# Linear attention with a maxout FFN on one core: a planner with other DMA times, other ranks, query exponentials in two steps

## The chip, the cores and the metric

The kernel runs on one core of a Trainium2 chip. The metric is the device time in microseconds (us) of one execution; the kernel before took 721.54 us, the median of three runs (720.34 to 723.81). The engines are named as the profile names them: PE (TensorE) with its weight loads PEld, DVE (VectorE), ACT (ScalarE), POOL (GpSimd), and SP, whose queue issues the DMAs.

## The reference

Eight batches of eight heads, 576 positions, head dimension 64, all in float32. Queries go through a softmax over the head dimension, keys through a softmax over the sequence. `kv` is a 64x64 matrix for each head, and the result, laid out as 4608 tokens x 512, goes through a maxout layer with three weight matrices and an output matrix.

```
q_s = exp(q - max(q, -1));  q_s /= sum(q_s, -1) + 1e-9
k_s = exp(k - max(k, seq)); k_s /= sum(k_s, seq) + 1e-9
kv  = einsum('bhsd,bhse->bhde', k_s, v)
x   = einsum('bhsd,bhde->bhse', q_s, kv)       -> 4608 x 512
h   = max(x @ w1, x @ w2, x @ w3)              w1..w3: 512 x 768
out = h @ w_out                                w_out: 768 x 512
```

## The kernel before, in words

**Work.** A pair is two heads of one batch: four pairs for each batch, 32 in all. For a pair the kernel takes the largest key of each column, exponentiates the keys, builds `kv` on PE (L489), scales it into a block-diagonal matrix (`bdf` for batches 0 and 1, `bdh` and `bdl` after; L505, L509), and multiplies the normalized queries by it (L639) into a piece of `x`: `x` for the first 512 positions, `left` for the 64 that remain. ACT casts the piece to its high part (L642) and DVE takes the low part (L644).

**Two kinds of batches.** Batches 0 and 1 are *turned*: PE transposes the keys (L419, L423), DVE reduces them (L428 to L430), ACT exponentiates (L434, L435), PE turns them back (L442, L444), ACT or DVE copies them out (L451); queries are transposed on PE (L612, L616) and copied into `qf` by ACT (L621, L623). Batches 2 to 7 are *plain*: DVE folds the keys (L459 to L461), POOL reduces over partitions (`kma`, L464), DVE subtracts (L467), ACT exponentiates (L474); queries turn by a DVE transpose and eight DMAs. A turned pair's queries are exponentiated either row by row on ACT (ten times an ACTIVATE of 128x64 and the read of its sum, L543; pairs in `Q_BY_ACT`), or by one subtraction (L548), one ACTIVATE of 128x640 (L563) and a sum on DVE (L565). L567, L568 and L571 normalize.

**FFN.** There are nine chunks of 512 token rows, one for each batch and one for the left-over rows. For a chunk there are 18 gate groups of four *trios* (a trio is three matmuls of 128x512, of low and high parts, L669), whose results ACT copies (L678) and DVE maximizes (L681); then ACT casts the high part of the hidden rows (L684), DVE takes the low part `h_l` (L687, a step that the planner may give to DVE or POOL), and 24 trios make the output (L707). The weights come as 24 slices of 512 KB of 64-bit numbers, each of which ACT, DVE and POOL turn into float parts (L320 to L348, POOL at L333); gate groups wait for their slice.

**Order.** The instructions' order on each engine is planned when the kernel is built. Every step of a stream names its engine, its cost in us and what it waits for (`Step`), and `Streams.run` gives each engine, whenever it comes free in the planner's clock, the ready step with the lowest rank. Ranks come from `AT`, `STEP`, `FIRST`, `CHUNK`, `SLICES_AT` and `SLICE_STEP`; the DMAs' times from the cost on SP (`"S"`), from `kb` and from `DMA_RATE`. At run time an engine works its list in that order and waits by semaphores. The small transposes, `kv` and left-over products of PE go through one PSUM tile `ps` of four quarters; the program's semaphores put all accesses to `ps` in the order in which they stand in the program. Gate groups go through four PSUM tiles `pf`.

Of the kernel before, what the change touches and what calls it, by code (L numbers as in the profile page):

```python
# [25 lines left out]
SIGNAL = 0.22  # L26
AHEAD = 0.5
DMA_LANDS = 2.0
DMA_RATE = 300.0
WAIT = 0.02  # L30

FIRST, CHUNK, SLICE = 27.0, 66.0, 2.7

AT = (7.3, 14.2, 18.2, 22.2, 39.0, 46.0, 63.0, 66.0)
STEP = (1.4, 2.8)
SLICES_AT, SLICE_STEP, SLICE_HI, SLICE_LO = 11.4, 0.18, 1.23, 1.56
# [41 lines left out]
class Streams:  # L78
# [16 lines left out]
    def ready(self, s, engine):  # L95
# [57 lines left out]

    def issue(self, t, e, c, s):
        step = s[4]
        end = t + c
        self.clock[e] = end
        if e in step.port:
            self.port = end
        if step.kb:  # L160
            self.queues = max(self.queues, end) + step.kb / DMA_RATE
            end = self.queues + DMA_LANDS
        s[3], s[5] = end, e
        if step.gives:
# [10 lines left out]
def linear_attention_then_maxout_ffn(  # L175
# [26 lines left out]
    nc = tc.nc  # L202
# [78 lines left out]
    st = Streams({"pf": 4, "pa": 3, "ps": 4, "keT": 1, "hp": NJ, "tmp": 3, "ke": 2, "qe": 2, "qf": 1, "qt": 2, "tb": 1, "qT": 2, "qhl": 1}, {"pf": in_pf})  # L281
    late_pools, turn_pools = [], []
    quarters = ps.tile([P, 4, P], F32, name="ps")
    small = (quarters[:, i % 4, :] for i in itertools.count())

# [66 lines left out]
    class Pair:  # L352
# [19 lines left out]
        def k_load(self):  # L372
            if self.b:
                prev = self.ago("ksub") if self.n >= NP + 2 else None
                if self.turned:
                    yield Step("S", 1.1, [prev], kb=256)
                    for hh in range(2):
                        nc.sync.dma_start(out=self.kt[:, 0:4, hh, :], in_=head_rows(k, self.b, 2 * self.g + hh))
                else:
                    yield Step("S", 0.55, [prev], kb=256)  # L380
                    nc.sync.dma_start(out=self.kt[:, :, 0:4, :], in_=main_rows(k, self.b, self.hs))
                yield Step("S", 0.5, gives=("k", self.n), kb=32)
                nc.sync.dma_start(
                    out=self.kt[0:LEFT, 4] if self.turned else self.kt[0:LEFT, :, 4, :], in_=left_rows(k, self.b, self.hs)
                )

        def v_load(self):
            if self.b:
                prev = self.ago("kv") if self.n >= NP + 2 else None
                for hh in range(2):  # L390
                    yield Step("S", 0.6, [prev], kb=128)
                    nc.sync.dma_start(out=self.vt[:, hh, 0:4, 0:D], in_=head_rows(v, self.b, 2 * self.g + hh))
                yield Step("S", 0.5, gives=("v", self.n), kb=32)
                nc.sync.dma_start(out=self.vt[0:LEFT, :, 4, 0:D], in_=left_rows(v, self.b, self.hs))

        def q_load(self):
            if self.b == 0:
                return
            if self.turned:
                prev = self.ago("qsub") if self.n >= NP + 2 else None  # L400
                self.qt = qbuf[self.m]
                yield Step("S", 0.55, [prev], kb=256)
                nc.sync.dma_start(out=self.qt[:, :, 0:4, :], in_=main_rows(q, self.b, self.hs))
                yield Step("S", 0.5, gives=("q", self.n), kb=32)
                nc.sync.dma_start(out=self.qt[0:LEFT, :, 4, :], in_=left_rows(q, self.b, self.hs))
            else:
                yield Step("S", 0.55, ["turn"], gives=("q", self.n), take=[("qt", self.n)], kb=288)
# [111 lines left out]
        def q_steps(self):  # L519
# [6 lines left out]
            if self.turned:  # L526
# [34 lines left out]
            if not by_act:  # L561
# [86 lines left out]
    class Chunk:  # L648
# [47 lines left out]
        def second(self, t):  # L696
# [38 lines left out]
    def first_loads():  # L735
# [143 lines left out]
```

## Time and profile before

| | us |
|---|---|
| median of three runs | 721.54 (720.34 to 723.81) |
| the profiled execution | 724.52 |
| its span in the trace | 722.4 |
| PE busy | 690.8 (96%) |
| DVE busy | 404.8 (56%) |
| ACT busy | 256.5 (36%) |
| POOL busy | 58.4 (8%) |

The profiled execution took 724.52 us, 3.0 more than the median; its trace spans 722.4 us. PE is the engine that is busy nearly throughout, so a wait of another engine counts only where PE waits for it. The stage up to 62.76 us holds most of PE's idle time.

### The profile page before, as it was taken

The page shows a single profiled execution, that of the slowest core. Times are in us where ns is not written, and L with a number is a line of the kernel's source. Part 1 is how long each engine was busy: PE and PEld are TensorE (multiplying, and loading weights), DVE is VectorE, ACT ScalarE, POOL GpSimd, SP SyncE. Part 2 cuts the span into 40 slices and gives each one's busy share as a digit, 9 for nine tenths or more (in the row PEclk, how much of TensorE's full clock was granted, in tenths as well). Part 3 has the DMA queues.
Part 4 walks back from the last instruction along what each step waited for, and adds up shares of the span by engine and source line. Part 5 has one row for each costly group of instructions (what it writes and reads, how often), then busy time and mean ns, then how long its engine had stood idle before and what let it go on. Part 6 is the DMA issues. An engine that isn't in the chain of part 4 may idle for free.

```text
span 722.4 us, 9841 instructions
## 1 busy us (share of the span) xinstructions
PE 690.8 (96%) x3528; PEld 553.5 (77%) x3528; DVE 404.8 (56%) x806; ACT 256.5 (36%) x610; POOL 58.4 (8%) x68
## 2 busy tenths in 40 slices
PE   3789999899999999999999999999999999999997
PEld 2557777677787887788878887888888888888886
DVE  6779997689988985675467646723222102211220
ACT  5878886333344324322342234212311111111111
POOL 2222432201000000000001000000000000000000
PEclk9989999999999999999999999999999999999999
DMA  7938414443445412530154005300100010000002
GB/s 212 257 110 252 134 61 135 141 104 99 110 125 155 113 46 69 143 109 1 33 146 126 18 25 149 83 1 10 66 1 0 15 44 0 1 33 26 1 0 59
DMA packets 86417, 58.07 MB, mean 80 GB/s; under 512 B 53344, under 2 KB 77920, under 8 KB 86368
## 3 DMA queue, kind: packets, MB, share of 16 engines
q1 hardware_dynamic: 86368, 57.44, 28.1%
q8 instruction: 28, 0.46, 0.3%
q14 instruction: 21, 0.17, 0.1%
HBM read 40.89 MB, written 9.44 MB: 70 GB/s over the span
## 4 chain that ended last, share of the span: by engine, by line
PE 85%; DVE 6%; DMA 3%; ACT 2%; SPq 2%; issue 1%; POOL 0%; DVEq 0%; ACTq 0%
PE pf L669 60%; PE pf L707 18%; PE ps L489 3%; PE pa L639 3%; ACT qe L543 1%; DMA kt<-in_k_dram 1%; PE ps L639 1%; DMA wst<-in_moe_w_dram 1%; SPq L589 1%; DVE ke L467 1%; PE pa L612 0%; DVE x L644 0%; DVE tb L576 0%; DMA qt<-in_q_dram 0%; SPq L757 0%
## 5 line engine op out<-in xcount | busy, mean ns | idle before, releaser
L669 PE MATMUL pf<-x,wh 128*128 128x512 f32 x1152 | 361.1, 395 | 1.1 <-DVE x L644 1.1
L669 PEld LDWEIGHTS pf<-x,wh 128*128 128x128 f32 x1152 | 218.0, 189 | 50.5 <-DVE x L644 1.7
L669 PE MATMUL pf<-x,wl 128*128 128x512 f32 x576 | 232.1, 403 | 0.9 <-ACT x L642 0.9
L681 DVE TENSOR_TENSOR m<-pf,m 128x512 f32<-128x512 f32 x108 | 74.3, 688 | 185.6 <-PE pf L669 185.0
L669 PEld LDWEIGHTS pf<-x,wl 128*128 128x128 f32 x576 | 109.2, 190 | 26.7 <-ACT x L642 1.1
L684 ACT CAST h_h<-m 128x512 fp32r<-128x512 f32 x54 | 33.5, 621 | 208.0 <-DVE m L681 208.0
L707 PE MATMUL pf<-ol,h_h 128*128 128x512 f32 x216 | 89.1, 412 | 0.0
L707 PE MATMUL pf<-oh,h_l 128*128 128x512 f32 x216 | 84.6, 392 | 0.0
L707 PE MATMUL pf<-oh,h_h 128*128 128x512 f32 x216 | 84.3, 390 | 0.0
L678 ACT COPY m<-pf 128x512 f32<-128x512 f32 x54 | 31.6, 586 | 52.2 <-PE pf L669 51.9
L687 DVE TENSOR_TENSOR h_l<-m,h_h 128x512 fp32r<-128x512 f32 x54 | 38.0, 704 | 20.7 <-ACT h_h L684 20.6
L707 PEld LDWEIGHTS pf<-ol,h_h 128*128 128x128 f32 x216 | 40.6, 188 | 9.0 <-issue 0.5
L707 PEld LDWEIGHTS pf<-oh,h_l 128*128 128x128 f32 x216 | 40.5, 188 | 8.9
L707 PEld LDWEIGHTS pf<-oh,h_h 128*128 128x128 f32 x216 | 40.7, 188 | 7.6 <-issue 0.5
L464 POOL PARTITION_ALL_REDUCE kma<-km x24 | 20.0, 832 | 305.3 <-DVE km L461 166.5
L669 PE MATMUL pf<-left,wh 128*128 128x512 f32 x144 | 44.3, 389 | 0.0
L712 ACT COPY m<-pf 128x512 f32<-128x512 f32 x36 | 21.1, 586 | 62.2 <-PE pf L707 61.3
L333 POOL TENSOR_TENSOR wst<-wx,wst 128x512 int32<-128x512 int32 x24 | 33.6, 1400 | 89.2 <-DVE wx L329 38.9
L576 DVE STREAM_TRANSPOSE tb<-qt 128x576 f32<-128x576 f32 x24 | 30.5, 1271 | 11.3 <-DMA qT<-tb 10.7
L669 PEld LDWEIGHTS pf<-left,wh 128*128 128x128 f32 x144 | 27.0, 188 | 5.6
L489 PEld LDWEIGHTS ps<-vt,ke 128*64 128x64 f32 (+1 forms) x560 | 18.9, 137 | 14.8 <-issue 5.0
L563 ACT ACTIVATE qt<-qt 128x576 f32<-128x576 f32 x24 | 16.5, 688 | 36.9 <-DVE qt L558 36.8
(110 smaller groups left out, 690.3 us busy)
## 6 DMA issues: line engine op xcount, KB each, us to landing
wst<-in_moe_w_dram SPq DMA_DIRECT2D x18, 512.0 KB, 4.2
out_dram<-m SPq DMA_DIRECT2D x32, 256.0 KB, 2.2
vt<-in_v_dram SPq DMA_DIRECT2D x56, 128.0 KB, 3.0
qt<-in_q_dram SPq DMA_DIRECT2D x24, 288.0 KB, 3.1
qT<-tb SPq DMA_DIRECT2D x192, 36.0 KB, 1.9
kt<-in_k_dram SPq DMA_DIRECT2D x24, 256.0 KB, 3.1
wst<-in_moe_w_out_dram SPq DMA_DIRECT2D x6, 512.0 KB, 3.3
q<-in_q_dram SPq DMA_DIRECT2D x8, 256.0 KB, 4.6
```

Source lines behind the costliest of these rows:

```text
L333: nc.gpsimd.tensor_add(out=low.bitcast(I32), in0=x.bitcast(I32), in1=low.bitcast(I32))
L464: nc.gpsimd.partition_all_reduce(kma, km, P, bass_isa.ReduceOp.max)
L489: nc.tensor.matmul(out=kv[r, :nv], lhsT=ke[rows, s, hh, :], rhs=self.vt[rows, hh, s, 0:nv], start=(s == 0), stop=(s == 4),)
L576: nc.vector.transpose(out=tb.rearrange("p e (c s) -> p s e c", s=QS), in_=self.qt.rearrange("p s (e c) -> p s e c", e=2))
L639: nc.tensor.matmul(out=xT, lhsT=l, rhs=r[:, cs], start=(i == 0), stop=(i == last))
L669: nc.tensor.matmul(out=ps, lhsT=l[:, cc, js], rhs=r, start=(cc == 0 and t == 0), stop=(cc == NC - 1 and t == 2))
L678: nc.scalar.copy(out=m, in_=self.m.pop((j, 0)))
L681: nc.vector.tensor_max(out=m, in0=self.m.pop((j, i)), in1=m)
L684: nc.scalar.copy(out=h, in_=m)
L687: unit[e].tensor_sub(out=lo, in0=m, in1=h.bitcast(F32))
L707: nc.tensor.matmul(out=po, lhsT=l, rhs=r[:, j, :], start=(j == 0 and i == 0), stop=(j == NJ - 1 and i == 2))
L712: nc.scalar.copy(out=o, in_=po)
```

## The change

All effective edits are to the planner's numbers, to the split of two steps, and to one PSUM ring. (1) DMA steps cost 0.64 us on SP for each DMA in place of 0.5 to 0.6; the planner's rate is 356 KB per us, and 0.62 of that up to 16 us, in place of 300; the left-over loads count as 50 KB and head-wise loads as 400 or 200. (2) The planner's engine clocks start at 0.72 to 4.0 us and not at 0. (3) `FIRST` goes from 27 to 22.7, `CHUNK` from 66 to 71.1, and `AT`, `STEP`, `SLICE_STEP` and `SLICE_HI` change. (4) The fourth pair's queries are loaded ahead of its keys, values and two weight slices. (5) Row-wise query exponentials are two steps of five rows. (6) Pairs 2 and 3 leave `Q_BY_ACT`. (7) Small PE results use three quarters of `ps` and not four; the fourth belongs to `keep_warm`, which with `WARM_TO` = 0 issues nothing.

```
-DMA_RATE = 300.0
+DMA_RATE, DMA_FIRST, DMA_AT_FIRST = 356.0, 0.62, 16.0
-FIRST, CHUNK, SLICE = 27.0, 66.0, 2.7
+WARM_FROM, WARM_TO, WARM_IDLE, WARM_COST = 4.2, 0.0, 0.3, 0.22
+FIRST, CHUNK, SLICE = 22.7, 71.1, 2.7
-AT = (7.3, 14.2, 18.2, 22.2, 39.0, 46.0, 63.0, 66.0)
-STEP = (1.4, 2.8)
+AT = (7.3, 14.2, 20.3, 22.2, 41.7, 48.7, 66.4, 62.3)
+STEP = (0.7, 3.92)
-FIRST_LOADS = 'kKqQvVwkqKQwvVkqwvkqvw'
+FIRST_LOADS = 'kKqQvVwkqKQwvVkqwqkvvw'
-Q_BY_ACT = (0, 1, 2, 3, 5, 6, 7)
+Q_BY_ACT = (0, 1, 5, 6, 7)
...
-        self.clock = dict.fromkeys("SAVGT-", 0.0)
+        self.clock = {"S": 0.72, "A": 2.2, "V": 4.0, "G": 3.0, "T": 0.0, "-": 0.0}
...
-            self.queues = max(self.queues, end) + step.kb / DMA_RATE
+            begun = max(self.queues, end)
+            self.queues = begun + step.kb / DMA_RATE / (DMA_FIRST if begun < DMA_AT_FIRST else 1.0)
...
-    small = (quarters[:, i % 4, :] for i in itertools.count())
+    small = (quarters[:, i % 3, :] for i in itertools.count())
...
-                    yield Step("S", 1.1, [prev], kb=256)
+                    yield Step("S", 1.28, [prev], kb=400)
...
-                    yield Step("A", rows * 0.33, take=[("qe", n)], gives=("qsub", n))
+                    yield Step("A", 5 * 0.33, take=[("qe", n)])
...
                     for hh in range(2):
+                        if hh:
+                            yield Step("A", 5 * 0.33, gives=("qsub", n))
                         for s in range(5):
...
-            yield Step("V", 0.28)
+            yield Step("V", 0.34)
```

Lines of the changed kernel stand 18 to 20 further down (L434 is L452, L543 is L563, L639 is L659, L669 is L689). Four places show what moves.

The first place is ACT's list from its first exponential on: `keT` are the turned keys, `qe` the queries, `wst` and `wh` a weight slice, `bdf` the scaled `kv`. Before:

```order
L543 ACTIVATE qe,qs_134<-q_98,qm_133 128x64 x10
L434 ACTIVATE keT,ks<-pa,km_217 128x512
L435 ACTIVATE keT,ks<-ps,km_217 128x64
L337 ACTIVATE wst<-wst 128x512
L341 CAST wh_79<-wx 128x4x128
L451 COPY ke<-pa 128x512
L451 COPY ke<-ps 64x128
L337 ACTIVATE wst<-wst 128x512
L621 COPY qf<-pa 128x512
L543 ACTIVATE qe,qs_136<-q_98,qm_135 128x64 x10
L341 CAST wh_80<-wx 128x4x128
```

And of the change, the same place:

```order
L452 ACTIVATE keT,ks<-pa,km_216 128x512
L453 ACTIVATE keT,ks<-ps,km_216 128x64
L563 ACTIVATE qe,qs_134<-q_98,qm_133 128x64 x5
L355 ACTIVATE wst<-wst 128x512
L563 ACTIVATE qe,qs_134<-q_98,qm_133 128x64 x5
L359 CAST wh_79<-wx 128x4x128
L523 ACTIVATE bdf_100<-ps,rk 64x64 x2
L563 ACTIVATE qe,qs_136<-q_98,qm_135 128x64 x5
L355 ACTIVATE wst<-wst 128x512
L641 COPY qf<-pa 128x512
L452 ACTIVATE keT,ks<-pa,km_303 128x512
L453 ACTIVATE keT,ks<-ps,km_303 128x64
```

The first keys' exponential (L434, now L452) moved ahead of the first queries', whose ten rows are now in two halves with a weight slice's step between, and the second `bdf` and `keT` no longer stand behind twenty rows.

The second place is PE about the third pair's `x` (`bdf_100`; `pa` and `ps` are the PSUM tiles of its 512 and 64 columns). Before:

```order
L639 MATMUL pa<-qf,bdf_100 128x512
L669 MATMUL pf<-x_86,wl_82 128x512
L669 MATMUL pf<-x_86,wh_79 128x512 x2
L442 MATMUL pa<-ident,keT 128x128 x4
L444 MATMUL ps<-ident,keT 64x128
L639 MATMUL ps<-qf,bdf_100 128x64
```

And of the change:

```order
L659 MATMUL pa<-qf,bdf_100 128x512
L659 MATMUL ps<-qf,bdf_100 128x64
L460 MATMUL pa<-ident,keT 128x128 x4
L462 MATMUL ps<-ident,keT 64x128
L632 MATMUL pa<-ident,qe 128x128 x4
L636 MATMUL ps<-ident,qe 128x64
```

The left-over product, which stood behind a trio and the next keys' transposes, now follows the main product directly.

The third place is PE at the first `kv` products of the plain batches (`vt0_92` and `vt1_93`, 128x65 in the trace; the number behind `pf` tells the gate group). Before:

```order
L489 MATMUL ps_130<-vt0_92,ke_1463 64x65 x10
L669 MATMUL pf_1482<-x1_756,wl0_82 128x512
L669 MATMUL pf_1482<-x1_756,wh0_79 128x512 x2
L669 MATMUL pf_1522<-x1_756,wl1_83 128x512
L669 MATMUL pf_1522<-x1_756,wh1_80 128x512 x2
L669 MATMUL pf_1522<-x1_756,wl1_83 128x512
L669 MATMUL pf_1522<-x1_756,wh1_80 128x512 x2
L489 MATMUL ps_130<-vt1_93,ke_1512 64x65 x10
```

And of the change:

```order
L507 MATMUL ps_130<-vt0_92,ke_1455 64x65 x10
L689 MATMUL pf_1468<-x1_712,wl0_82 128x512
L689 MATMUL pf_1468<-x1_712,wh0_79 128x512 x2
L689 MATMUL pf_1506<-x1_712,wl1_83 128x512
L689 MATMUL pf_1506<-x1_712,wh1_80 128x512 x2
L689 MATMUL pf_1506<-x1_712,wl1_83 128x512
L689 MATMUL pf_1506<-x1_712,wh1_80 128x512 x2
L689 MATMUL pf_1506<-x1_712,wl1_83 128x512
L689 MATMUL pf_1506<-x1_712,wh1_80 128x512 x2
L689 MATMUL pf_1506<-x1_712,wl1_83 128x512
L689 MATMUL pf_1506<-x1_712,wh1_80 128x512 x2
L507 MATMUL ps_130<-vt1_93,ke_1498 64x65 x10
```

Two more trios stand between the first and the second of these products.

The fourth place is POOL from the last clearing of buffers on (`kma` is the reduction over partitions, `h_l` the low part of hidden rows; ISA without names is a step that sets POOL up for the instruction that follows). Before:

```order
L789 MEMSET bdh_1435 128x128
L789 MEMSET bdl_1437 128x128
L789 MEMSET bdl_1439 128x128
L464 ISA
L464 ISA kma<-km 128x128 x24
```

And of the change:

```order
L482 ISA
L482 ISA kma<-km 128x128 x10
L707 ISA
L707 TENSOR_TENSOR h_l<-m,h_h 128x512
L482 ISA
L482 ISA kma<-km 128x128 x5
L707 ISA
L707 TENSOR_TENSOR h_l<-m,h_h 128x512
L482 ISA
L482 ISA kma<-km 128x128 x4
L707 ISA
L707 TENSOR_TENSOR h_l<-m,h_h 128x512
```

The 24 reductions stood in one row; now six `h_l` stand among them, five of them followed by a new set-up for the reductions, and each after a set-up of its own.

## Rows read from the trace of the kernel before

**Rows 1.** The page, parts 1 and 5: span, busy time, one group.

```profile
span 722.4 us, 9841 instructions
PE 690.8 (96%) x3528; PEld 553.5 (77%) x3528; DVE 404.8 (56%) x806; ACT 256.5 (36%) x610; POOL 58.4 (8%) x68
L687 DVE TENSOR_TENSOR h_l<-m,h_h 128x512 fp32r<-128x512 f32 x54 | 38.0, 704 | 20.7 <-ACT h_h L684 20.6
```

**Rows 2.** PE's waits, first 80 us: us in total, times, longest.

```profile
PE pa L442 <- ACT keT L434: 9.0, 2, 5.5
PE pa L419 <- DMA k<-in_k_dram: 4.5, 1, 4.5
PE ps L489 <- ACT qf L623: 2.8, 1, 2.8
```

**Rows 3.** Stretches: length, busy us by engine, granted clock, DMA share.

```profile
0.00:62.76 62.76, 41.68 (x239) 28.97 (x239) 47.74 (x118) 46.55 (x178) 16.33 (x23) 0.95 0.71 193
62.76:133.00 70.24, 70.24 (x362) 55.42 (x363) 59.86 (x117) 51.74 (x136) 22.14 (x22) 1.00 0.42 137
35.00:40.00 5.00, 2.24 (x23) 1.81 (x23) 4.25 (x10) 4.65 (x16) 1.19 (x1) 0.71 0.14 37
40.00:45.00 5.00, 4.78 (x16) 2.87 (x14) 2.69 (x9) 2.40 (x9) 0.10 (x1) 0.60 0.54 173
55.00:116.00 61.00, 60.15 (x339) 46.87 (x337) 58.78 (x110) 49.09 (x133) 19.82 (x14) 1.00 0.50 157
```

**Rows 4.** PE in order of time: start, length; idle before, releaser.

```profile
4.47 1.08 PE L419 MATMUL pa<-ident,k 128*128 128x128 f32 x4 [4.47 <-DMA k<-in_k_dram]
11.37 1.12 PE L442 MATMUL pa<-ident,keT 128*128 128x128 f32 x4 [5.51 <-ACT keT L434]
22.04 1.11 PE L442 MATMUL pa<-ident,keT 128*128 128x128 f32 x4 [3.50 <-ACT keT L434]
29.93 0.79 PE L669 MATMUL pf<-x,wl 128*128 128x512 f32 x1
37.98 1.54 PE L489 MATMUL ps<-v,ke 128*64 128x64 f32 x20 [2.76 <-ACT qf L623]
62.76 0.72 PE L669 MATMUL pf<-x,wh 128*128 128x512 f32 x2 [0.85 <-DVE x L644]
136.96 0.80 PE L489 MATMUL ps<-vt,ke 128*64 128x65 f32 x20 [1.67 <-ACT ke L474]
138.50 0.40 PE L669 MATMUL pf<-x,wl 128*128 128x512 f32 x1
139.19 0.39 PE L669 MATMUL pf<-x,wl 128*128 128x512 f32 x1
141.80 0.80 PE L489 MATMUL ps<-vt,ke 128*64 128x65 f32 x20 [1.76 <-ACT bdh L505]
295.44 0.30 PE L639 MATMUL ps<-q_l,bdh 128*128 128x64 f32 x1 [1.47 <-DVE bdl L509]
```

**Rows 5.** ACT in order of time, the first stage.

```profile
10.23 0.33 ACT L543 ACTIVATE qe<-q,qm 128x64 f32<-128x64 f32 x1
10.56 0.66 ACT L434 ACTIVATE keT<-pa,km 128x512 f32<-128x512 f32 x1
```

**Rows 6.** DVE in order of time: the start, the first plain pair.

```profile
7.11 0.68 DVE L428 TENSOR_REDUCE km<-pa 128x1 f32<-128x512 f32 x1
12.70 1.86 DVE L571 TENSOR_TENSOR qe<-qe,qs 128x640 f32<-128x640 f32 x1
20.91 0.82 DVE L571 TENSOR_TENSOR qe<-qe,qs 128x640 f32<-128x640 f32 x1
135.31 0.83 DVE L467 TENSOR_TENSOR ke<-kt,kma 128x640 f32<-128x640 f32 x1 [5.51 <-POOL kma L464]
```

**Rows 7.** POOL in order of time: its first slice and its first reduction.

```profile
12.58 1.29 POOL L333 TENSOR_TENSOR wst<-wx,wst 128x512 int32<-128x512 int32 x1 [9.59 <-DVE qs L567]
134.55 0.72 POOL L464 PARTITION_ALL_REDUCE kma<-km  x1 [5.82 <-issue]
```

More of the change, by code (lines that the diff above doesn't have):

```diff
@@ L28 @@
 DMA_LANDS = 2.0
-DMA_RATE = 300.0
+DMA_RATE, DMA_FIRST, DMA_AT_FIRST = 356.0, 0.62, 16.0
 WAIT = 0.02
-FIRST, CHUNK, SLICE = 27.0, 66.0, 2.7
-AT = (7.3, 14.2, 18.2, 22.2, 39.0, 46.0, 63.0, 66.0)
-STEP = (1.4, 2.8)
-SLICES_AT, SLICE_STEP, SLICE_HI, SLICE_LO = 11.4, 0.18, 1.23, 1.56
+WARM_FROM, WARM_TO, WARM_IDLE, WARM_COST = 4.2, 0.0, 0.3, 0.22
+FIRST, CHUNK, SLICE = 22.7, 71.1, 2.7
+AT = (7.3, 14.2, 20.3, 22.2, 41.7, 48.7, 66.4, 62.3)
+STEP = (0.7, 3.92)
+SLICES_AT, SLICE_STEP, SLICE_HI, SLICE_LO = 11.4, 0.29, 1.44, 1.56
 GATES_AT = 50.0
-FIRST_LOADS = 'kKqQvVwkqKQwvVkqwvkqvw'
+FIRST_LOADS = 'kKqQvVwkqKQwvVkqwqkvvw'
 ROOMS = 3, 2, 3, 4
-Q_BY_ACT = (0, 1, 2, 3, 5, 6, 7)
+Q_BY_ACT = (0, 1, 5, 6, 7)
 def dve(n):
@@ L121, in ready, with keep_warm @@
         return t
+    def keep_warm(self, t):
+        idle = t - max(self.clock["T"], WARM_FROM)
+        if t < WARM_TO and idle > WARM_IDLE:
+            self.fill(int((idle - WARM_IDLE) / WARM_COST) + 1)
     def advance(self, s, engine=None):
@@ L155, in issue @@
         step = s[4]
+        if e == "T":
+            self.keep_warm(t)
         end = t + c
@@ L280, in linear_attention_then_maxout_ffn, with fill @@
         in_pf += [(c, j, i) for j in range(NJ) for i in range(3)] + [(c, "y", t) for t in range(4)]
-    st = Streams({"pf": 4, "pa": 3, "ps": 4, "keT": 1, "hp": NJ, "tmp": 3, "ke": 2, "qe": 2, "qf": 1, "qt": 2, "tb": 1, "qT": 2, "qhl": 1}, {"pf": in_pf})
+    st = Streams({"pf": 4, "pa": 3, "ps": 3, "keT": 1, "hp": NJ, "tmp": 3, "ke": 2, "qe": 2, "qf": 1, "qt": 2, "tb": 1, "qT": 2, "qhl": 1}, {"pf": in_pf})
     late_pools, turn_pools = [], []
+    def fill(n):
+        for _ in range(n):
+            nc.tensor.matmul(out=idle, lhsT=ident, rhs=ident, start=True, stop=True)
+    st.fill = fill
     quarters = ps.tile([P, 4, P], F32, name="ps")
-    small = (quarters[:, i % 4, :] for i in itertools.count())
+    small = (quarters[:, i % 3, :] for i in itertools.count())
+    idle = quarters[:, 3, :]
     class Slice:
@@ L379, in k_load @@
                 else:
-                    yield Step("S", 0.55, [prev], kb=256)
+                    yield Step("S", 0.64, [prev], kb=256)
                     nc.sync.dma_start(out=self.kt[:, :, 0:4, :], in_=main_rows(k, self.b, self.hs))
-                yield Step("S", 0.5, gives=("k", self.n), kb=32)
+                yield Step("S", 0.64, gives=("k", self.n), kb=50)
                 nc.sync.dma_start(
@@ L390, in v_load @@
                 for hh in range(2):
-                    yield Step("S", 0.6, [prev], kb=128)
+                    yield Step("S", 0.64, [prev], kb=200)
                     nc.sync.dma_start(out=self.vt[:, hh, 0:4, 0:D], in_=head_rows(v, self.b, 2 * self.g + hh))
-                yield Step("S", 0.5, gives=("v", self.n), kb=32)
+                yield Step("S", 0.64, gives=("v", self.n), kb=50)
                 nc.sync.dma_start(out=self.vt[0:LEFT, :, 4, 0:D], in_=left_rows(v, self.b, self.hs))
@@ L401, in q_load @@
                 self.qt = qbuf[self.m]
-                yield Step("S", 0.55, [prev], kb=256)
+                yield Step("S", 0.64, [prev], kb=256)
                 nc.sync.dma_start(out=self.qt[:, :, 0:4, :], in_=main_rows(q, self.b, self.hs))
-                yield Step("S", 0.5, gives=("q", self.n), kb=32)
+                yield Step("S", 0.64, gives=("q", self.n), kb=50)
                 nc.sync.dma_start(out=self.qt[0:LEFT, :, 4, :], in_=left_rows(q, self.b, self.hs))
             else:
-                yield Step("S", 0.55, ["turn"], gives=("q", self.n), take=[("qt", self.n)], kb=288)
+                yield Step("S", 0.64, ["turn"], gives=("q", self.n), take=[("qt", self.n)], kb=288)
                 self.qt = turn_pools[0].tile([P, QS, D], F32, name="qt", bufs=2)
@@ L713, in second @@
             if c < B:
-                yield Step("S", 0.5, kb=256, free=[("tmp", (c, "y", t))], rank=-1000.0)
+                yield Step("S", 0.64, kb=256, free=[("tmp", (c, "y", t))], rank=-1000.0)
                 rows = out[c * S : c * S + CH, :]
@@ L721, in second @@
                 for i in range(2):
-                    yield Step("S", 0.5, kb=128, free=[("tmp", (c, "y", t))] if i else (), rank=-1000.0)
+                    yield Step("S", 0.64, kb=128, free=[("tmp", (c, "y", t))] if i else (), rank=-1000.0)
                     end = (2 * t + i + 1) * S
@@ L744, in first_loads @@
             if ch == "w":
-                yield Step("S", 0.6, gives=("wst", g), kb=512, take=[("wst", g)])
+                yield Step("S", 0.64, gives=("wst", g), kb=512, take=[("wst", g)])
                 slices[g].load(start, N_ST, N_X)
             elif ch == "k":
-                yield Step("S", 1.1, gives=("kmain", g), kb=256)
+                yield Step("S", 1.28, gives=("kmain", g), kb=400)
                 for h in (2 * g, 2 * g + 1):
@@ L751, in first_loads @@
             elif ch in to:
-                yield Step("S", 0.55, gives=("%smain" % ch, g), kb=256)
+                yield Step("S", 0.64, gives=("%smain" % ch, g), kb=256)
                 nc.sync.dma_start(out=to[ch][:, hs, 0:4, :], in_=main_rows(of[ch], 0, hs))
@@ L755, in first_loads @@
                 hs = slice(2, H) if g else slice(0, 2)
-                yield Step("S", 0.6, gives=(ch, g), kb=32 if g == 0 else 96)
+                yield Step("S", 0.64, gives=(ch, g), kb=50 if g == 0 else 150)
                 nc.sync.dma_start(out=to[low][0:LEFT, hs, 4, :], in_=left_rows(of[low], 0, hs))
@@ L794, in slice_load @@
     def slice_load(sl, late):
-        yield Step("S", 0.55, ["late"] if late else (), gives=("wst", sl.n), take=[("wst2" if late else "wst", sl.n)], kb=512)
+        yield Step("S", 0.64, ["late"] if late else (), gives=("wst", sl.n), take=[("wst2" if late else "wst", sl.n)], kb=512)
         sl.load(late_pools[0] if late else start, N_ST2 if late else N_ST, N_X2 if late else N_X)
```

## The prediction

> **What bounds the kernel now.** I read the page first, for the share of each engine: PE is busy for 690.8 of 722.4 us [rows 1], so 31.6 us is all that the order can win, unless a stretch at a lower granted clock goes too. The stretches tell where it lies: up to 62.76 us PE is busy for 41.68, which is 21.1 us idle; from there to 133 us it never waits [rows 3]. PE's waits name the causes of the first part: the keys' exponential `keT` on ACT, 9.0 us in two waits, the first keys' DMA, 4.5, and `qf` on ACT, 2.8 [rows 2]. The list of PE shows where: 5.51 before 11.37, 3.50 before 22.04, 2.76 before 37.98 [rows 4]. After 133 us there are 1.67 and 1.76 at the first plain pairs and 1.47 at 295.44 [rows 4]. The second thing to see is DVE between 55 and 116 us: 58.78 of 61.00 us busy [rows 3]. PE doesn't wait there, but DVE makes the weight slices, so a PE that comes earlier needs a DVE that comes earlier.
>
> **The start: what is won.** In the order of the change ACT's first exponential is `keT`, and DVE's first reduction is that of the keys. The first key transposes end near 4.47 + 1.08 = 5.6 [rows 4]; DVE's reductions take 0.68 [rows 6] and some 0.35 more, so `keT` starts near 6.7. It started at 10.56, behind ten rows of L543 whose last stands at 10.23 [rows 5]. PE began 0.81 after `keT` (11.37 against 10.56), so it begins at 7.5: 3.9 us earlier. For the second `keT` I add up ACT's list in the order's rows: a row of L543 begins 0.33 after the last (10.56 - 10.23), so five are 1.65; the first slice's word can't be had before its DMA, at about 10.2, as before. 10.2 + 0.65 + 1.65 + 0.65 (cast) + 0.65 (`bdf`) + 1.65 + 0.65 (the second slice's word) + 0.5 (`qf`) gives 16.6, with one small gap 16.85, and PE 0.81 later at 17.7, not 22.04. From there the PE list is the same down to the first trio: two products, the third keys' transposes, one `kv`. That is near 24.1 against 29.93: 5.8 us.
>
> **What stands in its place.** Up to 55 us I walked through the new lists with the traced durations. The 2.76 before 37.98 shrinks to 0.75, since `qf`'s left part no longer stands behind ten rows and four slice steps. New are 0.45 and 0.7 at the next two `kv`, and a large one: the third pair's left-over product, which follows the main one directly, waits for ACT's list (`qf` left, a slice's word and absolute values, the fourth `keT` in two parts), by my sum from 43.85 to 46.1, 2.25 us. Two more of 1.15 and 0.45 follow at 53.65 and 55.7, where five-row exponentials stand ahead of the next `keT`. These sum to 5.75, against 5.4 before for the same work, so dense work starts near 55.95. Since 0.6 us of key transposes less stand ahead of that point than of 62.76, the lead is 6.2 us.
>
> **What DVE takes back.** At 56 us DVE is only about 3.4 us ahead of its old list, and it has 1.1 us more to do until 110 us: a subtraction and a sum of 128x640, as long as L571 (0.82 [rows 6]), less what goes to POOL. The slack of slices shrinks from several us to about half a us, and I find waits of 0.5 and 0.9 in place of none. At the first plain `kv` PE also waits for POOL, which must end its slices before its first reduction; that reduction started 5.82 after POOL's last work [rows 7], and the change doesn't shorten it. I put that `kv` at 132.7, after a wait of 3.0, against 136.96 after 1.67: the lead is 4.3 there. It can't be below DVE's own, some 0.8 by then, nor above 5.6, if no slice is late.
>
> **Later.** Two trios more stand between the first and second plain `kv`. A trio is 0.69 (139.19 - 138.50), so of the 1.76 [rows 4] some 0.5 is left: 1.2 won (bounds 0 and 1.76). The plain pairs' products stand two to six trios later in PE's list, so I take 0.8 of the 1.47 at 295.44 [rows 4] as won (bounds 0 and 1.47, and a loss, the third rival).
>
> Contention of DVE and POOL costs: L571 took 1.86 at 12.70 while POOL's instruction of 12.58 ran, and 0.82 at 20.91, alone [rows 6, 7]. The change gives POOL a subtraction of 128x640 at about 23 us and six `h_l`. From 1.29 for 512 columns [rows 7] the first is 1.6, and DVE may lose up to that once. I take 1.0, bounds 0 and 1.6. The Trainium skill says, in "SBUF — State Buffer", section "Who interferes with whom", that a DVE instruction with two SBUF inputs and a POOL instruction that reads SBUF exclude each other for the whole instruction, whichever begins first. The trace agrees: 1.86 less 0.82 is about the 1.2 that POOL still had to run at 12.70. By that rule alone the term would be 1.6 when both meet and nothing when they don't.
>
> **The six `h_l` on POOL** I cost at nothing, and this is the least sure term. Each stands between two set-ups. The second kind has a price in the trace, at most 5.82 [rows 7]; the first has none, only the bound of 9.59 in which POOL also waited for work [rows 7]. What hides them: the closest place has a reduction, set-up, `h_l`, set-up and reduction, 0.7 + 5.8 + 1.3 + 5.8 + 0.7 = 14.3 us, if the first set-up is like the second, and the keys of the second reduction lie 33 matmuls, or 7.6 us, behind those of the first. DVE's subtraction behind that reduction then waits some 5.8 us, and the DVE maxima queued behind it are late by as much. Four gate results may stand in PSUM, each of twelve matmuls or 2.75 us, so PE feels it only from about 8 us on.
>
> The DMA numbers, the start clocks and the 0.34 change nothing at run time by themselves; the slices' first DMAs stand at the same place of SP's list. Three quarters of `ps` for four cost nothing that I can find, as accesses to it were in program order already.
>
> **Sum.** 4.3 + 1.2 + 0.8 - 1.0 = 5.3 us less than the profiled 724.52, 719.2. That execution lies 3.0 above the median, so the forecast is 721.54 - 5.3 = 716.2 us.
>
> **Rivals.** First, the lead is kept whole: no slice is late, the second plain wait and the mid waits go. 6.2 + 1.2 + 1.47 with a little from DVE's six `h_l` less is up to 9.9: 711.6. For it speaks that PE never waited from 62.76 to 133 [rows 3]; against it DVE's 96%.
>
> Second, DVE sets the pace: the lead falls to its 0.8, with 1.2 from the second `kv` is 2.0: 719.5. For it speaks the same 58.78 of 61.00; against, that ACT and POOL, not DVE, end the chain at 134.55.
>
> Third, slower: the set-ups around `h_l`. If each takes the whole 9.59, the closest place takes 21.9 us, DVE's subtraction is late by 7.5 more than above, 13.3 in all, and PE stands for about 5 us at each of the four places where two set-ups lie between reductions close together. That is 20 us at worst: 736. It is slower by over 0.5% once PE loses 8.9 / 4 = 2.2 at each, with set-ups of 8.3 us. For it: the first plain subtraction waited 5.51 for POOL [rows 6], and that one cost PE 1.67. Against: the first set-up may have been over long before 12.58. At its likelier price, 9 to 13 us, it gives 720 to 729; I write 726.
>
> Fourth, the clock. Behind the 2.76 idle at 37.98 the granted clock was 0.71 and then 0.60, the 1.2 GHz level for much of it [rows 3, 4]: 2.24 x 0.29 + 4.78 x 0.40 = 2.6 us of slower work. The 2.25 at 43.85 could do the same, while before only the one stretch was hit; with it the forecast is 718.8. The Trainium skill, "TensorE: Matmul & The Clock Gate", section "What's actually happening", states that the throttled state is the default and activity releases it; the trace agrees in that the clock fell after the longest gap. By that rule more gaps close together would keep the clock low, and the time would be this rival's.
>
> **Chances.** Forecast 0.42 (alone 713 to 719.5), whole lead 0.15, DVE's pace 0.19, set-ups 0.15, clock 0.09. About 0.5%, 3.6 us, is what a measurement of this kernel can tell from no change, so the bounds are 717.9 and 725.1. Faster: 0.34 of the forecast, 0.15, 0.02 and 0.02, together 0.53. Slower: 0.13 of the set-ups and 0.02 left over, 0.15. Same: 0.32. The range from 710.5 to 724.5 takes in all but most of the set-ups' case and a tail of the first rival.
>
> **What would show it.** `keT` first at 6.7 and the eT transposes at 7.5 and 17.7; the first trio near 24; a wait of about 2.2 before the left-over product at 46; dense PE from 56; the first plain `kv` near 132.7. DVE's subtractions waiting for POOL by 6 us or less with no wait of PE behind them would show the `h_l` hidden. A PE that waits for DVE maxima after 150 us, or a wait for a slice of over 2 us between 56 and 130, would make the prediction wrong.

## The result and the profile after

The changed kernel takes 725.14 us in the median of 20 runs (722.7 to 728.34), the kernel before 722.26 us (720.0 to 724.12): a ratio of 1.0039, 95% interval 1.0025 to 1.0053. It is slower by 2.9 us, where 716.2 was forecast and 710.5 to 724.5 given as the range. The difference is clear of the spread, but less than the 3.6 us that the prediction took as the least that can be told from no change. The profiled execution took 723.89 us, 1.2 less than the median, and that of the kernel before 2.3 more than its median, so of the two traces, 722.1 and 722.4 us long, the changed kernel's is the shorter.

Part 1 of the page of the changed kernel, beside [rows 1]:

```profile
span 722.1 us, 9826 instructions
PE 689.3 (95%) x3528; PEld 552.0 (76%) x3528; DVE 404.5 (56%) x801; ACT 252.6 (35%) x574; POOL 64.7 (9%) x75
```

PE's waits in the first 80 us (columns as in [rows 2]):

```profile
PE pa L460 <- ACT keT L452: 3.9, 3, 1.7
PE ps L659 <- ACT keT L453: 3.3, 1, 3.3
PE ps L441 <- ACT bdf L523: 2.5, 1, 2.5
```

The two waits of 9.0 us for `keT` are down to 3.9 in three; two new ones stand in the `ps` tile, for `keT` (3.3) and `bdf` (2.5). PE's list shows where, beside [rows 4]:

```profile
7.47 1.11 PE L460 MATMUL pa<-ident,keT 128*128 128x128 f32 x4 [1.69 <-ACT keT L452]
15.20 0.37 PE L441 MATMUL ps<-ident,k 64*128 64x64 f32 x1 [2.50 <-ACT bdf L523]
18.83 1.12 PE L460 MATMUL pa<-ident,keT 128*128 128x128 f32 x4 [1.21 <-ACT keT L452]
24.62 0.50 PE L689 MATMUL pf<-x,wl 128*128 128x512 f32 x1
45.00 0.43 PE L659 MATMUL ps<-qf,bdf 128*128 128x64 f32 x2 [3.28 <-ACT keT L453]
53.56 0.65 PE L460 MATMUL pa<-ident,keT 128*128 128x128 f32 x4 [0.98 <-ACT keT L452]
132.85 1.35 PE L507 MATMUL ps<-vt,ke 128*64 128x65 f32 x20 [2.62 <-ACT ke L492]
```

The keys' transposes begin at 7.47 and not at 11.37, the first trio at 24.62 and not at 29.93, and after 53.56 PE is dense, where it was from 62.76. The first trio's row takes 0.50 and not 0.79: PE runs at the higher level of its clock already, which adds to the lead. The stretches after that, beside [rows 3]:

```profile
55.00:116.00 61.00, 59.47 (x314) 46.09 (x313) 56.48 (x109) 47.28 (x126) 19.60 (x14) 1.00 0.50 153
133.00:145.00 12.00, 12.00 (x73) 9.54 (x74) 9.17 (x22) 4.15 (x9) 0.70 (x1) 0.75 0.53 146
399.00:404.50 5.50, 0.43 (x3) 0.11 (x1) 2.63 (x7) 0.13 (x1) 0.72 (x1) 0.77 0.00 0
404.00:409.00 5.00, 4.60 (x11) 3.66 (x12) 4.86 (x11) 1.78 (x3) 0.00 (x0) 0.52 0.00 0
```

DVE is busy for 56.48 of 61.00 us, less than before. From 133 to 145 us PE is busy throughout, at a mean granted clock of 0.75. The last two rows are new: 5.50 us with hardly any work on PE, and a stretch at 0.52 behind it.

How far PE is ahead is read from ACT's copies of the FFN's results, which both kernels make in the same number. Before, the first copy of a gate group, and three places where outputs are copied:

```profile
63.74 0.57 ACT L678 COPY m<-pf 128x512 f32<-128x512 f32 x1
131.18 1.27 ACT L712 COPY m<-pf 128x512 f32<-128x512 f32 x2 [3.29 <-PE pf L707]
374.56 0.59 ACT L712 COPY m<-pf 128x512 f32<-128x512 f32 x1
428.55 0.59 ACT L712 COPY m<-pf 128x512 f32<-128x512 f32 x1 [0.55 <-PE pf L707]
```

And the same four after (a row takes in the copies that follow each other without a gap):

```profile
55.95 0.59 ACT L698 COPY m<-pf 128x512 f32<-128x512 f32 x1
126.12 1.95 ACT L732 COPY m<-pf 128x512 f32<-128x512 f32 x3 [2.61 <-PE pf L727]
366.70 0.59 ACT L732 COPY m<-pf 128x512 f32<-128x512 f32 x1 [0.46 <-PE pf L727]
428.32 0.59 ACT L732 COPY m<-pf 128x512 f32<-128x512 f32 x1 [0.55 <-PE pf L727]
```

The lead is 7.8 us at the first copy, 5.1 at the outputs of 126.12, 7.9 at that of 366.70, and 0.2 at that of 428.32. So it was won at the start, fell, came back, and was lost between 367 and 428 us. A copy is a rough mark, because other work of PE stands differently between the copies. Two places are exact, as PE has worked off the same number of matmuls there: the outputs of 131.18 (126.12 after), and the gate group's copy of 385.27 (377.65 after). Up to these places, before first, after second (columns as in [rows 3], the number behind x is that of instructions):

```profile
0.00:131.18 131.18, 110.10 (x592) 82.89 (x593) 107.60 (x233) 96.65 (x311) 38.47 (x44) 0.97 0.56 164
0.00:385.27 385.27, 358.24 (x1970) 281.78 (x1971) 297.56 (x620) 189.04 (x488) 54.90 (x64) 0.99 0.43 122
```

```profile
0.00:126.12 126.12, 106.05 (x592) 78.80 (x593) 110.11 (x234) 92.45 (x275) 39.27 (x45) 1.00 0.59 171
0.00:377.65 377.65, 354.41 (x1970) 278.83 (x1971) 296.99 (x615) 184.47 (x451) 55.97 (x66) 0.99 0.44 123
```

At the first place PE has stood idle for 21.08 us before and 20.07 after. Only 1.0 of the lead of 5.1 is waiting that went; the other 4.0 is PE's own busy time, 106.05 in place of 110.10 for the same matmuls, as more of them ran at the higher level of the clock: the granted clock before was 0.71 and 0.60 from 35 to 45 us [rows 3], and 1.00 after. At the second place the lead is 7.6 us, 3.8 of waiting and 3.8 of busy time.

This is PE where the lead is lost:

```profile
398.71 0.61 PE L689 MATMUL pf<-x,wh 128*128 128x512 f32 x2
404.40 0.80 PE L689 MATMUL pf<-x,wl 128*128 128x512 f32 x1 [5.07 <-DVE m L701]
404.99 1.05 PE L689 MATMUL pf<-x,wh 128*128 128x512 f32 x2
406.27 1.05 PE L689 MATMUL pf<-x,wh 128*128 128x512 f32 x2
```

It waits 5.07 us for a DVE maximum, and its next trios take 1.28 us each (406.27 less 404.99, the 1.2 GHz level) where 0.69 is usual. POOL and DVE in the same place:

```profile
377.96 1.28 POOL L707 TENSOR_TENSOR h_l<-m,h_h 128x512 fp32r<-128x512 f32 x1 [6.75 <-issue]
385.77 0.72 POOL L482 PARTITION_ALL_REDUCE kma<-km  x1 [6.53 <-issue]
393.89 1.30 POOL L707 TENSOR_TENSOR h_l<-m,h_h 128x512 fp32r<-128x512 f32 x1 [7.40 <-DVE qm L576]
401.05 0.72 POOL L482 PARTITION_ALL_REDUCE kma<-km  x1 [5.86 <-issue]
```

```profile
386.53 0.83 DVE L485 TENSOR_TENSOR ke<-kt,kma 128x640 f32<-128x640 f32 x1 [3.56 <-POOL kma L482]
392.29 0.29 DVE L479 TENSOR_TENSOR km<-km,kt 128x128 f32<-128x128 f32 x1
394.56 0.92 DVE L477 TENSOR_TENSOR kh<-kt 128x256 f32<-128x256 f32 x1
401.81 0.29 DVE L478 TENSOR_TENSOR km<-kh 128x128 f32<-128x128 f32 x1 [6.33 <-POOL kma L482]
402.34 0.75 DVE L585 TENSOR_REDUCE qs<-qt 128x9 f32<-128x576 f32 x1
403.66 0.68 DVE L701 TENSOR_TENSOR m<-pf,m 128x512 f32<-128x512 f32 x1
```

POOL stands idle for 6 to 7 us before each of its four instructions and waits for nothing that takes that long: 6.75 and 7.40 before the `h_l`, 6.53 and 5.86 before the reductions. DVE's L478 writes `km`, of which there is one buffer, and POOL's reduction of 401.05 has to read the `km` finished at 392.58 (392.29 + 0.29) first. So DVE stands for 6.33 us, then has two reductions of L585 and L576 ahead of the maximum of 403.66, and PE, whose four result tiles are full since 399, begins at 404.40.

### The profile page after: what moved, and what is told of

Same layout as the page of the kernel before. It is cut to its first block, busy times and chain, and to the rows that moved or that the text cites. A ratio compares the mean times of both kernels' runs of the same rounds, so it can differ in the third digit from the quotient of the medians.

```text
span 722.1 us, 9826 instructions
## 1 busy us (share of the span) xinstructions
PE 689.3 (95%) x3528; PEld 552.0 (76%) x3528; DVE 404.5 (56%) x801; ACT 252.6 (35%) x574; POOL 64.7 (9%) x75
## 4 chain that ended last, share of the span: by engine, by line
PE 84%; DVE 5%; issue 3%; ACT 2%; SPq 2%; DMA 2%; POOL 1%; DVEq 0%; POOLq 0%; ACTq 0%
PE pf L689 55%; PE pf L727 20%; PE pa L659 3%; PE ps L507 3%; SPq L609 1%; PE ps L659 1%; DMA kt<-in_k_dram 1%; DVE tb L596 1%; DMA wst<-in_moe_w_dram 1%; PE pa L460 1%; DMA qT<-tb 1%; DVE m L701 0%; ACT qe L563 0%; DVE qm L576 0%; POOL h_l L707 0%
## 5 line engine op out<-in xcount | busy, mean ns | idle before, releaser
L689 PE MATMUL pf<-x,wh 128*128 128x512 f32 x1152 | 361.4, 395 | 0.0
L689 PEld LDWEIGHTS pf<-x,wh 128*128 128x128 f32 x1152 | 218.6, 190 | 48.8 <-issue 0.5
L689 PE MATMUL pf<-x,wl 128*128 128x512 f32 x576 | 231.6, 402 | 5.9 <-DVE m L701 5.2
L689 PEld LDWEIGHTS pf<-x,wl 128*128 128x128 f32 x576 | 109.4, 190 | 32.7 <-DVE m L701 6.1
L707 DVE TENSOR_TENSOR h_l<-m,h_h 128x512 fp32r<-128x512 f32 x48 | 33.1, 690 | 21.3 <-ACT h_h L704 21.3
L689 PE MATMUL pf<-left,wh 128*128 128x512 f32 x144 | 44.4, 389 | 0.0
L482 POOL PARTITION_ALL_REDUCE kma<-km x24 | 17.7, 738 | 282.7 <-DVE km L479 143.8
L485 DVE TENSOR_TENSOR ke<-kt,kma 128x640 f32<-128x640 f32 x24 | 19.6, 815 | 24.6 <-POOL kma L482 24.6
L689 PEld LDWEIGHTS pf<-left,wh 128*128 128x128 f32 x144 | 27.0, 188 | 5.6
```

Source lines behind the costliest of these rows:

```text
L485: nc.vector.tensor_tensor(out=ke.rearrange("p s h d -> p h s d"), in0=kt, in1=kma.rearrange("p (h d) -> p h d", h=2).unsqueeze(2).broadcas ...
L689: nc.tensor.matmul(out=ps, lhsT=l[:, cc, js], rhs=r, start=(cc == 0 and t == 0), stop=(cc == NC - 1 and t == 2))
L707: unit[e].tensor_sub(out=lo, in0=m, in1=h.bitcast(F32))
```

## The experiments

All ratios are to the kernel before, run on the same chip in the same rounds.

**All `h_l` on DVE** (e1), **and five of six left on POOL** (e2). The marks behind `#` say which run a line is of; `...` stands for what is left out.

```
-            e = yield Step("VG", (0.61, 1.28), gives=("h", c, j), free=[("tmp", (c, j))], port="VG")
+            e = yield Step("V", 0.61, gives=("h", c, j), free=[("tmp", (c, j))], port="V")      # e1
+            e = yield Step(*(("G", 1.28) if (c, j) in ((2, 0), (3, 0), (4, 0), (5, 0), (5, 1))  # e2
+                else ("V", 0.61)), gives=("h", c, j), free=[("tmp", (c, j))], port="VG")
```

Expected of e1: 

> The changed kernel with all 54 low parts h_l of the hidden rows on DVE, so that POOL works through its 24 reductions with one set-up. Theory (the set-ups around (4,0) and (4,1) hold DVE, and through it PE, once): the 5.07 us wait at 404 us and the slow stretch behind it, together 7.6 us, go; about 725.1 - 7.6 = 717.5 us, ratio to before 0.993. Rival one (the loss is the low clock at 133 to 145 us and the waits of the start, and the POOL wait only fills a gap that something else would take): 724 to 725, ratio 1.002 to 1.004. Rival two (all six places cost, the others by way of DVE): below 715.

Expected of e2: 

> The changed kernel with five of its six h_l left on POOL and only that of chunk 4, hidden block 1, on DVE. Theory (only two h_l with a single reduction between them cost PE anything): as good as all on DVE, about 717.5 us, ratio 0.993, with DVE still waiting 3 to 6 us for reductions elsewhere. Rival (each set-up costs PE a share): between the changed kernel and all on DVE, 718.8 to 724. Where it is the adjacent pair (5,0) and (5,1), 460 to 475 us, that comes next in tightness, a new wait of PE stands there.

e1 took 718.63 us, ratio 0.9943 (0.9923 to 0.9964), e2 717.9 us, 0.9927 (0.9898 to 0.9955). PE waits nowhere between 300 and 450 us in e1, and in e2, where DVE still waits 19.4 us in all for reductions after 146 us, up to 6.0 at once, the one wait for a maximum is 0.2. So a single `h_l` of 54, that of chunk 4 and block 1, took the kernel from some 718 to 725 us; the other five cost nothing that can be measured. Rival two of e1 and the rival of e2 fall. From 133 to 145 us PE is slowed in e1 as well (granted 0.72, and 2.9 us of waiting at the first plain `kv`), so rival one falls too.

**The two `h_l` in the kernel before** (e3), forced to POOL as in e2, for chunk 4, blocks 0 and 1.

```
+            e = yield Step(*(("G", 1.28) if (c, j) in ((4, 0), (4, 1)) else ("V", 0.61)), ...
```

Expected: 

> The kernel before with only the two h_l of chunk 4, blocks 0 and 1, on POOL. Theory: the same double set-up around one reduction arises, DVE waits some 6 us for it and PE loses up to 5 us and some clock: 724 to 730 us, ratio 1.002 to 1.010. Rival (the place in the changed kernel is bad for another reason): no change, ratio within 0.002 of 1.

It took 722.59 us, ratio 0.9995 (0.998 to 1.0011): no change, so that expectation of mine failed. POOL shows what is different:

```profile
391.27 0.72 POOL L464 PARTITION_ALL_REDUCE kma<-km  x1 [5.86 <-issue]
398.98 1.83 POOL L687 TENSOR_TENSOR h_l<-m,h_h 128x512 fp32r<-128x512 f32 x1 [6.99 <-issue]
426.71 0.73 POOL L464 PARTITION_ALL_REDUCE kma<-km  x1 [25.90 <-DVE ke L467]
```

The set-ups are there, but behind the second `h_l` of 398.98 no reduction was due until 426.71, so DVE was held once only, 3.4 us, and PE waits for no maximum between 300 and 450 us. Set-ups are not enough: a reduction has to follow that DVE waits for.

**Two buffers for `km`** (e5), each engine's order as in the changed kernel, all six `h_l` on POOL.

```
-            km = turn_pools[0].tile([P, 2 * D], F32, name="km", bufs=1)
+            km = turn_pools[0].tile([P, 2 * D], F32, name="km", bufs=2)
```

Expected: 

> The changed kernel, each engine's order untouched and all six h_l on POOL, with two buffers for km (what DVE hands to POOL's reduction) in place of one. Theory: PE's 5.07 us wait at 404 comes by DVE's km (L478), which may not write the one buffer before POOL's delayed reduction has read it, and holds the maxima behind it; with two buffers DVE goes on and the wait goes, though POOL's set-ups stay: 717 to 719 us, ratio 0.993 to 0.995. Rival (DVE is held by its subtraction for the delayed reduction, or PE by the h_l itself): the wait stays within 1 us and the time at 724 to 726.

717.17 us, ratio 0.9924 (0.99 to 0.9949). POOL, and DVE beside it:

```profile
379.09 1.28 POOL L707 TENSOR_TENSOR h_l<-m,h_h 128x512 fp32r<-128x512 f32 x1 [7.26 <-issue]
386.36 0.72 POOL L482 PARTITION_ALL_REDUCE kma<-km  x1 [6.00 <-issue]
395.55 1.28 POOL L707 TENSOR_TENSOR h_l<-m,h_h 128x512 fp32r<-128x512 f32 x1 [8.46 <-DVE kh L477]
402.53 0.72 POOL L482 PARTITION_ALL_REDUCE kma<-km  x1 [5.71 <-issue]
```

```profile
395.59 1.39 DVE L478 TENSOR_TENSOR km<-kh 128x128 f32<-128x128 f32 x1
398.54 0.68 DVE L701 TENSOR_TENSOR m<-pf,m 128x512 f32<-128x512 f32 x1
```

POOL comes as late as before, its reduction at 402.53, but DVE's L478 at 395.59 doesn't wait for it, the maximum of 398.54 is in time, and PE's 5.07 is gone; one wait for a maximum is left, 1.5 us at 315. All four engines work in the order of the changed kernel, and its DVE waits for a reduction with a `km` only this once, so the second buffer had nothing else to win there. That is the cause shown by itself: the loss went through the one `km` buffer.

**The first reduction's set-up told to the planner** (e6), with all `h_l` on DVE.

```
-            yield Step("G", 0.8, [("ksub", n - 1)], gives=("kmt", n))
+            yield Step("G", 6.5 if n == TURNED * NP else 0.8, [("ksub", n - 1)], gives=("kmt", n))
```

Expected: 

> The changed kernel with all h_l on DVE and the planner told that the first reduction costs POOL 6.5 us and not 0.8, so that some nine trios and not three stand ahead of the first plain kv. Theory: the 2.6 to 2.9 us wait at that kv and the stretch at the lower clock behind it (granted 0.72 to 0.75 from 133 to 145 us, some 3 us) both go: 718.6 - 5.5 = 713 us, ratio 0.987. Rival (the wait goes elsewhere, since the plain batches' x comes later): 717 to 719.

712.01 us, ratio 0.9865 (0.9842 to 0.9889), the best kernel here, better than both. The first plain `kv` and the stretch:

```profile
136.64 0.80 PE L507 MATMUL ps<-vt,ke 128*64 128x65 f32 x20
```

```profile
133.00:145.00 12.00, 12.00 (x85) 9.38 (x85) 9.95 (x23) 3.97 (x8) 1.77 (x2) 1.00 0.36 88
```

There is no wait, and the granted clock is 1.00 where it was 0.75, and 0.72 in e1. That is 6.6 us less than e1 by the medians and 5.6 by the two ratios (e1 ran in other rounds), from only four executions.

**The same in the kernel before** (e9), by the same edit of its line of that step.

Expected: 

> The kernel before with all h_l on DVE (where they are already) and the planner told that the first reduction costs POOL 6.5 us, so that seven more trios stand ahead of the first plain kv. Theory: its waits of 1.67 and 1.76 us at 137 and 142 us and the slow stretch behind them (granted 0.80 and 0.86 from 140 to 150 us, some 2 us) go without any of the change: 717 to 718.5 us, ratio 0.993 to 0.995. Rival (the plain batches' chain is needed that early, so the wait moves on): 721 to 723.

717.21 us, ratio 0.9936 (0.9911 to 0.9961). Its waits at 137 and 142 us are gone, while that of 295.44 stays, with 1.6 at 289.68. This one number is worth 4.5 us without any of the change.

**Parts of the change undone**, all with `h_l` on DVE: FIRST and CHUNK as before (e4), AT and STEP (e7), Q_BY_ACT (e8); and, with the set-up planned as in e6, the rows in one step of ten (e10) and the old first loads (e11).

```
-FIRST, CHUNK, SLICE = 22.7, 71.1, 2.7
+FIRST, CHUNK, SLICE = 27.0, 66.0, 2.7                                # e4
-AT = (7.3, 14.2, 20.3, 22.2, 41.7, 48.7, 66.4, 62.3)
-STEP = (0.7, 3.92)
+AT = (7.3, 14.2, 18.2, 22.2, 39.0, 46.0, 63.0, 66.0)                 # e7
+STEP = (1.4, 2.8)                                                    # e7
-Q_BY_ACT = (0, 1, 5, 6, 7)
+Q_BY_ACT = (0, 1, 2, 3, 5, 6, 7)                                     # e8
-                    yield Step("A", 5 * 0.33, take=[("qe", n)])
+                    yield Step("A", rows * 0.33, take=[("qe", n)], gives=("qsub", n))  # e10
-FIRST_LOADS = 'kKqQvVwkqKQwvVkqwqkvvw'
+FIRST_LOADS = 'kKqQvVwkqKQwvVkqwvkqvw'                               # e11
```

In e10 the second step of five rows is gone as well.

Expected of e4: 

> The changed kernel with all h_l on DVE and FIRST and CHUNK back at 27.0 and 66.0, so that the ranks of the plain batches are those of before. Theory: the win is that of the start, and the ranks of plain batches carry none of it: 717 to 719 us. Rival (the ranks of the plain batches hold part of the lead, by the 1.47 us wait at 295 us of before and the first plain pairs): 720 to 722, with such waits in the trace.

Expected of e7: 

> The changed kernel with all h_l on DVE and AT and STEP as before. Theory (these ranks put the first keys' exponential and reductions ahead of the queries' and win most of the start): first trio at 28 to 30 us, 721 to 723 us. Rival (the start clocks, the DMA times and the split already do it): first trio before 26 us and 717 to 720 us.

Expected of e8: 

> The changed kernel with all h_l on DVE and pairs 2 and 3 back among those whose queries are exponentiated row by row on ACT. Theory (ACT's rows stand ahead of the third and fourth keys' exponentials between 25 and 55 us): PE waits 2 to 4 us more there, 720 to 722 us. Rival (DVE, which gets back two sums and a subtraction, sets the pace): equal or faster, 716 to 718.6.

Expected of e10: 

> The changed kernel with all h_l on DVE and the first reduction's set-up planned (the kernel of 712 us), but the row-wise exponentials in one step of ten rows. Theory (the two halves let a slice's word and the second keys' exponential in between): 714 to 717 us, the second keT and the first trio 1 to 3 us later. Rival (the split costs nothing and wins nothing): 711.5 to 713.

Expected of e11: 

> The kernel of 712 us with the first loads in the order of before, the fourth pair's queries behind its keys, values and two slices. Theory (the fourth pair isn't waited for by its queries): no change, 711.5 to 713.5. Rival (its queries' exponential comes late): 714 or more, with a PE wait for the fourth pair's query transposes between 45 and 60 us.

| | us | ratio | against |
|---|---|---|---|
| e4 | 718.14 | 0.9932 (0.9906 to 0.9959) | e1 718.63 |
| e7 | 720.64 | 0.9973 (0.9959 to 0.9986) | e1 718.63 |
| e8 | 723.06 | 1.0016 (1.0002 to 1.003) | e1 718.63 |
| e10 | 714.28 | 0.9893 (0.987 to 0.9917) | e6 712.01 |
| e11 | 713.01 | 0.9879 (0.9855 to 0.9903) | e6 712.01 |

e4: the ranks of the plain batches carry none of the win. e7 came between its theories: its first trio stands at 25.50, so the early part isn't won by AT and STEP, as the rival said. What it lost afterwards is not waiting: `keT` on ACT takes 6.0 us in four waits, but in all PE stands idle for 27.3 us, and for 28.5 in e1. PE's busy time is 692.3 us against 688.6, and the granted clock stood at 0.50 from 35 to 50 us.

e8 is as its theory said, and more. PE stands at the query transposes behind ACT's ten rows, and the granted clock is 0.54 from 30 to 40 us:

```profile
31.64 0.37 PE L636 MATMUL ps<-ident,qe 64*128 64x64 f32 x1 [5.00 <-ACT keT L453]
```

Pairs 2 and 3 leaving the row-wise list is the largest of the parts that were undone by themselves, 4.4 us. e10 took some 2 us more than e6, and the intervals just overlap. Its second keys' transposes come 3.2 us later (22.01, and 18.78 in e6), as its theory said, but its first trio comes no later (24.41, and 24.64), and PE waits less in all; so what the split is worth isn't shown. e11: within what can be told from no change; the old loads cost nothing that shows. The DMA numbers, the start clocks, the slices' ranks and the three quarters of `ps` were not undone by themselves, so no run tells what each is worth.

## Why the prediction was wrong

**The start** was near in its times, and its lead was in part luck. `keT` was put at 6.7 and the transposes at 7.5: 6.64 and 7.47. The second transposes were put at 17.7 and stand at 18.83; a wait of 2.50 in the `ps` tile for `bdf` at 15.20 was missing from my list. The first trio came at 24.62 (24.1), the wait at the third pair's left-over product was 3.28 and not 2.25, and dense work began at 54 and not at 56. The lead of 6.2 was 7.8 at the first copy. But only 2.5 of that is less waiting (PE idle for 21.08 us up to there before, 18.54 after). Nearly all of the rest is PE's busy time, shorter by the clock, and for a clock that stands higher the prediction had no term.

**What DVE takes back** came in size and not in kind. I had put down waits of 0.5 and 0.9 for weight slices. PE's waits from 63 to 133 us that weren't the first plain `kv` sum to 1.5, but they are for `qf` (0.7), `left` (0.6) and `km` (0.2), none for a slice. The `kv` itself was put at 132.7 after 3.0 and stands at 132.85 after 2.62. The lead was put at 4.3 there; by the terms that the prediction names, 6.2 less 0.5, less 0.9 and less the 1.33 by which the wait grows, it would have been 3.5. It was 5.1 just ahead of the `kv`. The second rival, DVE's pace with a lead of 0.8, is out. The 1.0 for contention, which was in the sum, shows in no wait of PE for DVE of that length.

**Later:** the second plain `kv` has no wait at all (0.5 was forecast), but the trios between the two ran at the lower level: the first four take 5.15 us (134.13 to 139.28), 2.4 more than four times 0.69. The wait at 295 is gone altogether, and the lead at 377.65 us is 7.6, not far from the 8.9 that the first rival keeps.

**The step that failed** is "The six `h_l` on POOL I cost at nothing", by "PE feels it only from about 8 us on". The set-ups had nearly the price I took: 5.7 to 7.4 where I had 5.8, so that the closest place took 16.0 us (385.77 to 401.77) and not 14.3. What I missed is what DVE waits with. I followed its subtraction behind the reduction, which waited 3.56 at 386.53, and stopped there; at the second `h_l`, that of chunk 4 and block 1, the next instruction of DVE that touches what the late reduction reads is the next pair's L478, and DVE was held a second time, 6.33, fifteen us after the first, with its list already late and two long reductions ahead of the maximum. Taking one hold of 5.8 against 8 us of room was the error: the room is that of a maximum that would otherwise be on time. e5, with the order unchanged, shows it. A PE that waits for DVE maxima after 150 us was one of the signs by which the prediction said that it would be wrong. The third rival had the place and the kind of loss (a PE that waits for DVE maxima), but asked for set-ups of 8.3 us and for four places; one place sufficed, at 5.07 and about 2 us of clock. (Its 9 to 13 us on top of 716.2 give 725 to 729, not the 720 to 729 that stand there.)

**The clock rival** didn't come where it was put, in this execution: after the 3.28 us of the third pair's product the granted clock stayed at 1.00. It did come behind 5.07 and behind 2.62. And in e1, whose order is the same up to there, it came behind 3.28 at the same place (granted 0.66 from 45 to 55 us), so the profiled execution was a lucky one there. The longest gap of which that rival speaks is the longest after the clock had risen: the 5.51 before 11.37 was longer, but the transposes on both sides of it take 1.1 us, against 0.65 at 53.56 in the changed kernel, so it lies before the rise.

**The sum with the right sizes:** 5.1 us stood at 126.12 (1.0 of waiting and 4.0 of busy time), 7.6 at 377.65, and of these 7.4 went at 404 (the wait of 5.07, and some 2.1 of lower clock in the trios behind it): 0.2, as the spans say, 722.4 and 722.1. Without the step that failed, in e1, e2 and e5, the time is 717.2 to 718.6 where 716.2 was forecast, so the other terms came out near as a sum, though not one by one. The medians lie 2.9 us apart and these two spans 0.3 the other way, and that goes with the clock: the seven runs of the changed kernel with a mean granted clock of 0.991 or more, the profiled one among them, have a median of 723.7 us, the eight of 0.987 or less 726.5. The kernel before ran at 0.992 to 0.994 in the mean, in the rounds of the experiments; against the seven alone, 1.4 of the 2.9 are left. What makes the clock differ between executions of one program stays open.

## What to carry to other kernels

When a planner may give a step to another engine, price what the engine does between instructions of different kinds: here 6 to 7 us of set-up before an instruction of 1.3 us, and as much again behind it. To see whether a late engine is hidden, follow every instruction that touches its operands, also those that only want the buffer back, and count the holds on one queue together. A cost that the planner has wrong is worth more than a rank: one number gave 4.5 us in the kernel before and some 6 in this one. And when a lead is measured, split it into waiting and busy time at a place where the same work is done: of the 5.1 us here only 1.0 was waiting.

## What the runs showed of the hardware that was not expected

POOL's set-up shows in the trace only as idle time: 5.69 before the first reduction, 5.70 to 6.53 on each of the five returns to it, 6.7 to 7.4 before each of the six `h_l`. In nine of these twelve the trace names nothing that POOL waited for. The Trainium skill, "GPSIMD Engine Reference", section "2.1 Instruction dispatch", gives some 6 us for the first call of a newly loaded kernel, with no instruction of its own in the profile. The trace agrees before the reductions; before an `h_l` it shows somewhat more, and it shows the gap on every change in both directions.

The same gap doesn't always lower the clock. After 3.28 us of idle at 45 us the changed kernel ran on at 1.00; after 3.28 us at the same place of the same order e1 was granted 0.66. This is e1's row, to be read beside that of 45.00 above:

```profile
44.95 0.43 PE L659 MATMUL ps<-qf,bdf 128*128 128x64 f32 x2 [3.28 <-ACT keT L453]
```

And from 45 to 55 us, the changed kernel first and e1 second (columns as in [rows 3]):

```profile
45.00:55.00 10.00, 8.95 (x61) 6.54 (x62) 8.92 (x21) 9.79 (x38) 3.73 (x3) 1.00 0.63 188
```

```profile
45.00:55.00 10.00, 10.00 (x51) 7.13 (x51) 7.53 (x17) 7.55 (x30) 3.67 (x3) 0.66 0.60 182
```

POOL's subtraction of 128x640 took 1.26 us (at 20.76 us), no more than its other instructions of 512 columns, against the 1.6 I had worked out. Beside it, at 20.85, DVE's L587 of 128x10 took 1.20 and ended with it; at 37.95, with no instruction of POOL beside it, it took 0.17.
